# One tile of a pre-LayerNorm block: a transpose on TensorE in place of one by DMA

## The chip, the cores and the metric

The kernel runs on one core of a Trainium2 chip. Its time is the device time of one execution in microseconds; below, "the trace" is one execution recorded by the hardware profiler. Engines are TensorE (PE; its weight loads are listed as PEld), VectorE (DVE), ScalarE (ACT), GpSimd (POOL) and SyncE (SP, which issues most of the DMAs).

## The reference

```python
h  = x + A(layernorm(x))          # linear attention, 32 heads of 32
h2 = h + B(layernorm(h))          # gated ReLU MLP

# A: q, k, v = split(x @ wqkv);  phi(t) = where(t > 0, t + 1, exp(t)) + 1e-6
#    kv = phi(k)^T v ;  z = sum_s phi(k)
#    o  = (phi(q) kv) / (phi(q) z + 1e-6) ;  A = o @ wo
# B: (relu(x @ W_gate) * (x @ W_up)) @ W_down
```

`x` is 1 x 2048 x 1024, `W_gate` and `W_up` are 1024 x 3584, `W_down` is 3584 x 1024, all in bfloat16.

## The kernel before

Tokens are cut into 16 tiles of 128. `order` lists them in two halves of eight: tiles 0 to 3 and 8 to 11 first, then 4 to 7 and 12 to 15. A half has two blocks `hnT[s][0]` and `hnT[s][1]` of 512 tokens each, because the products of the MLP are done by one level of the Strassen-Winograd scheme, seven products in place of eight, for which the two token blocks and the two halves of the feature chunks make a 2 x 2 split. In what follows a tile is named by its place n in `order`, so "tile 7" is `order[7]`, the last of the first half.

The attention's second part goes through each tile in five stages (`attn_stages`): `nd` multiplies by kv and z and divides (matmuls at L511, ScalarE's Ln and Exp at L515 and L517, VectorE's product at L518); `oT` transposes the result by DMA (L525); `x_in` loads the residual (L529); `wo_h` multiplies by `wo` (L541), adds the residual (L543), stores h (L546) and normalises it into the row `hn` (L551 to L557, the last a 128x1024 activation on ScalarE); `hn_T` transposes that row into `hnT` (L560), where the MLP needs the features on the partitions. `LAG = (0, 1, 1, 2, 4)`: at step t the stages of tiles t, t-1, t-1, t-2 and t-4 are written, in this order. The rows `hn` have two buffers.

For the tiles of the second token block, `attn_step` then writes four sums on VectorE (`left_sums`, L117 to L120) that the Strassen products read: `hs` and the rewritten part of `hn`. From step 8 on, four "quads" of the MLP (`early_quad`, products at L705) are woven in between the remaining attention steps: the first product of the first quad at step 8, all others after step 11. A quad's products go to PSUM tags A (two buffers), D (one) and E (two); D is the second product (L705 `Dq`, read by L714). Stage `wo_h` of tiles 6 to 9 borrows tag E, the others take tag `ab`, which has three buffers and is shared with `nd`.

Up to here the order of each engine's instructions is not the order of the code: they are placed by a scheduler when their inputs are ready, earlier code first. After the four quads, the order on PE, VectorE and ScalarE is written out by hand (`quad`, L785 and following).

At the start of the kernel a similar step exists: the first four tiles of the normalised x are transposed by PE (`transpose_in`, L283) into tag D, four 128x128 blocks at a time, and copied to SBUF by VectorE or ScalarE (L284).

Of the kernel before, what the change touches and what calls it, by code (L numbers as in the profile page):

```python
# [10 lines left out]
BF16 = mybir.dt.bfloat16  # L11
# [20 lines left out]
def block_kernel(ctx: ExitStack, tc: tile.TileContext, x, wqkv, wo, wg, wu, wd, out, H: int):  # L32
    nc = tc.nc
    P = 128
    xf = x.flatten_outer_dims()
    of = out.flatten_outer_dims()
    S, D = xf.shape
# [4 lines left out]
    KC = D // P  # L42
# [5 lines left out]
    KH = KC // 2  # L48
# [9 lines left out]
    ident = consts.tile([P, P], BF16, name="ident")  # L58
# [146 lines left out]
    order = [(i * HS + s * SW) // P + tt for s in range(NS) for i in range(2) for tt in range(NT)]  # L205
# [5 lines left out]
    pspool = psctx.enter_context(tc.tile_pool(name="ps", bufs=1, space=PSUM))  # L211
    with ExitStack() as actx:
# [208 lines left out]
        for c in range(KC):  # L421
            bnk, i = divmod(c, GPB)
# [41 lines left out]
    hnT, hns = [], []  # L464
# [32 lines left out]
    def attn_stages(t):  # L497

        i, r = divmod(t * P, HS)
        s, r = divmod(r, SW)  # L500
        st = {}

        def nd():
            o_sb = bwork.tile([P, D], BF16, tag="o_sb", name="o_sb")
            st["o"] = o_sb
            held.append(o_sb)
            ov = o_sb[:].rearrange("p (k h e) -> p k h e", k=KC, h=HPC)
            for c0, n in pieces:
                ps = ndpool.tile([P, NW], FP32, tag="ab", name="nd")
                for c in range(c0, c0 + n):  # L510
                    nc.tensor.matmul(ps[:, (c - c0) * NDW:(c - c0 + 1) * NDW], lhsT=pqT[:, c, t * P:(t + 1) * P],  # L511
                                     rhs=kvz[:, c, :], start=True, stop=True)
                ndv = ps[:, 0:n * NDW].rearrange("p (k w) -> p k w", w=NDW)
                den = bsmall.tile([P, GPB, HPC], FP32, tag="den", name="den")
                nc.scalar.activation(out=den[:, 0:n], in_=ndv[:, :, P:NDW], func=ACT.Ln, bias=deps[:], scale=1.0)  # L515
                rd = bsmall.tile([P, GPB, HPC], FP32, tag="rd", name="rd")
                nc.scalar.activation(out=rd[:, 0:n], in_=den[:, 0:n], func=ACT.Exp, scale=-1.0)  # L517
                nc.vector.tensor_tensor(  # L518
                    out=ov[:, c0:c0 + n], in0=ndv[:, :, 0:P].rearrange("p k (h e) -> p k h e", h=HPC),
                    in1=rd[:, 0:n, :].unsqueeze(3).to_broadcast([P, n, HPC, Dh]), op=ALU.mult)  # L520

        def oT():
            oT = bwork.tile([P, D], BF16, tag="oT", bufs=XB, name="oT")
            st["oT"] = oT[:].rearrange("p (c t) -> p c t", c=KC)
            nc.sync.dma_start_transpose(out=st["oT"], in_=st["o"][:])  # L525

        def x_in():
            x_sb = bwork.tile([P, D], BF16, tag="x_res", bufs=XB, name="x_res")
            nc.sync.dma_start(out=x_sb[:], in_=xf[t * P:(t + 1) * P, :])  # L529
            st["x"] = x_sb  # L530

        def wo_h(borrow):
            h_sb = st["x"]
            tot = bsmall.tile([P, 2], FP32, tag="tot", name="tot")
            for j in range(2):
                if borrow:
                    ps = pspool.tile([P, NW], FP32, tag="E", bufs=2, name="attn")
                else:
                    ps = abpool.tile([P, NW], FP32, tag="ab", name="attn")
                for c in range(KC):  # L540
                    nc.tensor.matmul(ps[:], lhsT=st["oT"][:, c, :], rhs=wo_sb[:, c, j * NW:(j + 1) * NW],  # L541
                                     start=(c == 0), stop=(c == KC - 1))
                nc.vector.scalar_tensor_tensor(out=h_sb[:, j * NW:(j + 1) * NW], in0=ps[:], scalar=1.0,  # L543
                                               in1=h_sb[:, j * NW:(j + 1) * NW], op0=ALU.mult, op1=ALU.add,
                                               accum_out=tot[:, j:j + 1])
            nc.sync.dma_start(out=h_dram[i][s][:, r // P, :], in_=h_sb[:])  # L546
            st["hn"] = bwork.tile([P, D], BF16, tag="hn", bufs=HB, name="hn")

            sm = bsmall.tile([P, 6], FP32, tag="sm", name="sm")
            nmean, var, lnv, rstd, nmr = (sm[:, i:i + 1] for i in range(5))  # L550
            nc.vector.tensor_scalar(out=nmean, in0=tot[:, 0:1], scalar1=tot[:, 1:2], scalar2=-1.0 / D,  # L551
                                    op0=ALU.add, op1=ALU.mult)
            nc.scalar.activation(out=st["hn"][:], in_=h_sb[:], func=ACT.Square, bias=nmean, scale=1.0, accum_out=var)  # L553
            nc.scalar.activation(out=lnv, in_=var, func=ACT.Ln, bias=LN_EPS, scale=1.0 / D)
            nc.scalar.activation(out=rstd, in_=lnv, func=ACT.Exp, scale=-0.5)
            nc.scalar.activation(out=nmr, in_=nmean, func=ACT.Identity, scale=rstd)
            nc.scalar.activation(out=st["hn"][:], in_=h_sb[:], func=ACT.Identity, bias=nmr, scale=rstd)  # L557

        def hn_T():
            nc.sync.dma_start_transpose(out=hnT[s][i][:, :, r:r + P], in_=st["hn"][:])  # L560

        return nd, oT, x_in, wo_h, hn_T

    LAG = (0, 1, 1, 2, 4)
    STS = ST // NS
# [163 lines left out]
    for f in range(NE):  # L729
        st = {}  # L730
# [149 lines left out]
    for r, (wt, f, fi, toks) in enumerate(runs):  # L880
        w = [ops() for _, ops in now]
        later = []
        for n, s in enumerate(toks):
# [51 lines left out]
            if k == nwin - 3:  # L935
                for x in range(2):
                    t = wpools[1].tile([P, KC * 2 * GP * P], BF16, tag=("wg", "wu")[x], name="wd")
# [16 lines left out]
    for n in range(2):  # L954
        t = fpool.tile([P, 4 * D], BF16, tag="wraw", bufs=2, name="xd")
# [242 lines left out]
    for n in range(1, len(OUTER)):  # L1198
# [73 lines left out]
        else:  # L1272
            pss = []
            for p in range(4):
# [13 lines left out]
                s, t0 = divmod(2 * p, NT)  # L1288
# [55 lines left out]
```

## Time and profile before

| | us |
|---|---|
| median of 4 runs | 743.79 (742.24 to 744.88) |
| profiled execution | 744.27 |
| its span, first to last instruction | 742.50 |
| PE busy | 726.7 (98%) |
| VectorE busy | 563.3 (76%) |
| ScalarE busy | 322.1 (43%) |
| DMA issues of `hn` transposes | 16, median 3.7 from issue to landing |

A row of the page or of a timeline names the line of the code, the engine, the operation, and `out<-in` by the program's names. In a timeline the bracket at the end of a row is the time that the engine idled before it, and what ended that. In a table of stretches each engine has its busy time and the number of its instructions, and "PEclk" is the TensorE clock that was granted, 1.00 being the full one.

### The profile page before, as it was taken

Reading aid. Unit: us, or ns where it says so; the run is one execution under the profiler, and the core shown is the slowest. Engines: PE = TensorE matmul, PEld = TensorE weight load, DVE = VectorE, ACT = ScalarE, POOL = GpSimd, SP = SyncE. Lnnn points to the kernel's source line nnn. Section 1 sums busy time; section 2 is a strip of 40 time slices with the busy share of each in tenths; the row PEclk is TensorE's granted clock in tenths of the full one; section 3 lists DMA queues with packets and bytes.
Section 4 is the critical chain, followed back from the end, with each engine's and each line's share of the span. In section 5 each row is a group of like instructions: output and inputs, shape, how many; then the busy total and the mean of one; then the engine's idle time right before and its main releaser. Section 6 shows DMA issues by size and latency. Waiting matters only on the chain.

```text
span 742.5 us, 10623 instructions
## 1 busy us (share of the span) xinstructions
PE 726.7 (98%) x4020; PEld 382.5 (52%) x4020; DVE 563.3 (76%) x991; ACT 322.1 (43%) x580; POOL 5.7 (1%) x44
## 2 busy tenths in 40 slices
PE   8999999999989999999999999999999999999997
PEld 3444555444434444444444444444444458888566
DVE  6998653676987667778778777877787469996797
ACT  4786653878686655444443434443445120000000
POOL 0000000000000000000000000000000000000000
PEclk9999999999999999999999999999999999999999
DMA  9765003079796525164647349475574399988822
GB/s 317 167 140 156 0 1 111 4 162 235 163 212 158 134 79 186 49 191 125 203 134 219 123 164 305 158 207 207 178 265 133 116 393 355 319 289 300 298 77 80
DMA packets 146579, 132.03 MB, mean 178 GB/s; under 512 B 50912, under 2 KB 128096, under 8 KB 146528
## 3 DMA queue, kind: packets, MB, share of 16 engines
q1 hardware_dynamic: 135392, 123.23, 55.1%
q10 hardware_dynamic: 11136, 8.13, 3.4%
q8 instruction: 31, 0.51, 0.3%
q14 instruction: 20, 0.16, 0.1%
HBM read 79.95 MB, written 39.85 MB: 161 GB/s over the span
## 4 chain that ended last, share of the span: by engine, by line
PE 78%; DVE 8%; ACT 7%; DMA 5%; issue 1%; SPq 0%; DVEq 0%; POOL 0%; ACTq 0%
PE accA L785 22%; PE accY L785 8%; PE accX L785 8%; PE accA L1117 8%; PE Aq L298 3%; PE accA L946 3%; PE accX L1117 3%; PE Aq L438 3%; PE accY L1117 2%; PE attn L541 2%; DMA hn<-hn 2%; PE Aq L705 2%; PE Eq L298 2%; PE accY L946 2%; PE accX L946 2%; ACT hn L553 1%
## 5 line engine op out<-in xcount | busy, mean ns | idle before, releaser
L795 ACT ACTIVATE gu<-gu 128x512 bf16<-128x512 bf16 x72 | 45.4, 630 | 131.4 <-DVE gu L794 131.4
L790 ACT COPY snap<-accA 128x1024 f32<-128x1024 f32 x72 | 72.5, 1008 | 36.4 <-PE accA L785 36.3
L785 PEld LDWEIGHTS <-tg 128*128 128x128 f16 x384 | 37.6, 98 | 45.3
L785 PEld LDWEIGHTS <-tu 128*128 128x128 f16 x384 | 37.6, 98 | 45.3
L541 PE MATMUL attn<-wo_mem,oT 128*128 128x512 bf16 x256 | 58.6, 379 | 1.1 <-DMA oT<-o_sb 0.6
L794 DVE TENSOR_TENSOR gu<-accY,snap 128x1024 bf16<-128x1024 f32 x36 | 43.9, 1220 | 10.0 <-ACT snap L790 10.0
L785 PE MATMUL accA<-hn,tg 128*128 128x512 f16 (+1 forms) x192 | 49.3, 379 | 0.0
L785 PE MATMUL accA<-hn,tu 128*128 128x512 f16 (+1 forms) x192 | 49.3, 379 | 0.0
L154 ACT COPY u<-Aq 128x512 f32<-128x512 f32 x56 | 32.4, 582 | 38.5 <-PE Aq L298 19.2
L794 DVE TENSOR_TENSOR gu<-accX,snap 128x1024 bf16<-128x1024 f32 x36 | 43.9, 1220 | 6.3 <-PE accX L785 3.7
L1117 PEld LDWEIGHTS <-x 128*128 128x128 f16 (+1 forms) x448 | 43.8, 98 | 5.5
L785 PEld LDWEIGHTS <-wg 128*128 128x128 bf16 x288 | 28.2, 98 | 34.0
L785 PEld LDWEIGHTS <-wu 128*128 128x128 bf16 x288 | 28.2, 98 | 34.0
L541 PEld LDWEIGHTS <-oT 128*128 128x128 bf16 x256 | 24.7, 98 | 31.3 <-issue 3.1
L798 DVE TENSOR_TENSOR hq<-gu 128x512 bf16<-128x512 bf16 x48 | 20.3, 423 | 14.3 <-ACT gu L795 14.2
L298 PEld LDWEIGHTS <-xT 128*128 128x128 bf16 (+1 forms) x192 | 18.6, 98 | 23.6 <-issue 2.2
L1117 PEld LDWEIGHTS <-xs 128*128 128x128 f16 x280 | 27.4, 98 | 3.2
L543 DVE SCALAR_TENSOR_TENSOR x_res<-attn,x_res 128x512 bf16<-128x512 f32 x32 | 21.8, 688 | 8.6 <-PE attn L541 8.6
L946 PEld LDWEIGHTS <-x 128*128 128x128 bf16 (+1 forms) x168 | 16.4, 98 | 19.6
L518 DVE TENSOR_TENSOR o_sb<-nd,rd 128x384 bf16<-128x384 f32 (+1 forms) x48 | 22.8, 508 | 4.6 <-ACT rd L517 4.5
L1123 DVE TENSOR_TENSOR snap<-accA,u 128x1024 f32<-128x1024 f32 x16 | 19.5, 1221 | 8.3 <-PE accA L1117 8.1
L785 PE MATMUL accA<-hs,tg 128*128 128x512 f16 x96 | 24.6, 379 | 0.0
(232 smaller groups left out, 1407.8 us busy)
## 6 DMA issues: line engine op xcount, KB each, us to landing
x<-x_dram SPq DMA_DIRECT2D x17, 896.0 KB, 8.0
x_dram<-hq SPq DMA_DIRECT2D x28, 512.0 KB, 3.2
wg<-in_B_W_gate_dram SPq DMA_DIRECT2D x14, 512.0 KB, 5.2
wu<-in_B_W_up_dram SPq DMA_DIRECT2D x14, 512.0 KB, 7.3
wraw<-in_B_W_down_dram SPq DMA_DIRECT2D x14, 512.0 KB, 5.1
x_dram<-hq SPq DMA_DIRECT2D x28, 256.0 KB, 2.7
t_dram<-wt SPq DMA_DIRECT2D x28, 256.0 KB, 2.2
xd<-x_dram SPq DMA_DIRECT2D x6, 896.0 KB, 7.1
```

The costliest lines, as they stand in the source:

```text
L154: nc.scalar.copy(out=snaps[nm, v], in_=A[v][:])
L298: nc.tensor.matmul(ps[:], lhsT=left[m - 1][:, kc, r + v * P:r + (v + 1) * P], rhs=right[m - 1][:, kc, :], start=(start and kc == 0), stop= ...
L438: nc.tensor.matmul(ps[:], lhsT=rq[m - 1][:, kc, (c + v) * P:(c + v + 1) * P], rhs=left[m - 1][:, kc, :], start=(start and kc == 0), stop=( ...
L518: nc.vector.tensor_tensor(out=ov[:, c0:c0 + n], in0=ndv[:, :, 0:P].rearrange("p k (h e) -> p k h e", h=HPC), in1=rd[:, 0:n, :].unsqueeze(3 ...
L541: nc.tensor.matmul(ps[:], lhsT=st["oT"][:, c, :], rhs=wo_sb[:, c, j * NW:(j + 1) * NW], start=(c == 0), stop=(c == KC - 1))
L543: nc.vector.scalar_tensor_tensor(out=h_sb[:, j * NW:(j + 1) * NW], in0=ps[:], scalar=1.0, in1=h_sb[:, j * NW:(j + 1) * NW], op0=ALU.mult, ...
L785: nc.tensor.matmul(ps[:, v, :], lhsT=w[v][n - 1][:, kc, :], rhs=left[n - 1][:, kc, :], start=(t is not None and kc == 0), stop=(kc == KH - ...
L790: nc.scalar.copy(out=st[nm][:], in_=halves(st["A"]))
L794: add(out=g[:], in0=halves(st[nm]), in1=st[base][:], op=ALU.add)
L795: nc.scalar.activation(out=g[:, 0, :], in_=g[:, 0, :], func=ACT.Relu)
L946: nc.tensor.matmul(ps[:, t * NW:(t + 1) * NW], lhsT=x_tile(n, s, kh)[:, f, (t0 + t) * P:(t0 + t + 1) * P], rhs=w_tile(n, kh)[:, f, :], sta ...
L1117: nc.tensor.matmul(pv[:, tt, :], lhsT=left(m)[:, f, tt * P:(tt + 1) * P], rhs=right(m)[:, f, :], start=(t is not None and f == 0 and tt % ...
```

## The change

For tile 7 alone, `hn_T` no longer issues a DMA transpose. PE transposes the row's eight 128x128 blocks into one PSUM tile of tag D, ScalarE copies the first four blocks into `hnT` and VectorE the last four. The other fifteen tiles keep their DMA transposes.

```diff
         def hn_T():
+            if t == order[STS - 1]:
+                pt = pspool.tile([P, KC, P], BF16, tag="D", bufs=1, name="tp")
+                for kc in range(KC):
+                    nc.tensor.transpose(pt[:, kc, :], st["hn"][:, kc * P:(kc + 1) * P], ident[:])
+                nc.scalar.copy(out=hnT[s][i][:, 0:KH, r:r + P], in_=pt[:, 0:KH])
+                nc.vector.tensor_copy(out=hnT[s][i][:, KH:KC, r:r + P], in_=pt[:, KH:KC])
+                return
             nc.sync.dma_start_transpose(out=hnT[s][i][:, :, r:r + P], in_=st["hn"][:])
```

## The prediction

> **What bounds the kernel now.** I read the page first, then the stretch table around the edited step, then TensorE's, SyncE's, ScalarE's and VectorE's timelines there, and last the chain of waits. On the page TensorE (PE) is busy 726.7 of 742.5 us, so a change gains only by closing a hole in PE's stream or by raising its clock. The table of stretches shows where a hole is (columns: length, then busy time of PE, weight loads, VectorE, ScalarE, GpSimd, then granted clock, DMA share, GB/s):
>
> ```profile
> 216.95:220.34 3.39, 0.68 (x7) 0.37 (x5) 2.83 (x10) 3.26 (x11) 0.00 (x0) 1.00 0.94 258
> 220.34:223.73 3.39, 2.98 (x8) 1.05 (x8) 3.39 (x10) 1.91 (x6) 0.00 (x0) 0.50 0.97 236
> 223.73:293.00 69.27, 67.51 (x327) 30.80 (x326) 49.22 (x121) 41.09 (x94) 0.00 (x0) 1.00 0.53 139
> 293.00:600.00 307.00, 307.00 (x1424) 139.18 (x1423) 227.15 (x415) 127.26 (x170) 0.00 (x0) 1.00 0.56 176
> ```
>
> PE works 0.68 of 3.39 us, and then 3.39 us pass at a granted clock of 0.50. Afterwards there is always other work: 1.76 us idle up to 293, none up to 600. What is won or lost near 220 is therefore kept to the end. PE's timeline (start, length, instructions, idle time before them in brackets):
>
> ```profile
> 207.79 0.38 PE L705 MATMUL Dq<-hn,wg 128*128 128x512 bf16 x1
> ...
> 212.75 0.59 PE L705 MATMUL Dq<-hn,wg 128*128 128x512 bf16 x2
> 213.23 3.61 PE L541 MATMUL attn<-wo_mem,oT 128*128 128x512 bf16 x16
> 216.68 0.34 PE L511 MATMUL nd<-kvz,pq_mem 128*128 128x132 bf16 x3
> 217.21 0.34 PE L511 MATMUL nd<-kvz,pq_mem 128*128 128x132 bf16 x3 [0.19 <-DVE o_sb L518]
> 218.55 0.28 PE L511 MATMUL nd<-kvz,pq_mem 128*128 128x132 bf16 x2 [1.00 <-DVE o_sb L518]
> 220.75 1.01 PE L705 MATMUL Eq<-hs,tg 128*128 128x512 f16 x2 [1.93 <-DVE hs L117]
> ```
>
> The hole is 0.19 + 1.00 + 1.93 = 3.12 us, and its largest part ends with the first Strassen sum (L117) of the first half's last tile, tile 7 in the order. SyncE, ScalarE and VectorE say why that sum is late:
>
> ```profile
> 216.14 1.46 SPq L560 DMA_TRANSPOSE hn<-hn  x1
> ...
> 212.47 1.24 ACT L557 ACTIVATE hn<-x_res,sm 128x1024 bf16<-128x1024 bf16 x1
> ...
> 218.42 1.24 ACT L557 ACTIVATE hn<-x_res,sm 128x1024 bf16<-128x1024 bf16 x1
> ...
> 219.02 0.69 DVE L543 SCALAR_TENSOR_TENSOR x_res<-attn,x_res 128x512 bf16<-128x512 f32 x1
> ...
> 220.27 0.43 DVE L117 TENSOR_TENSOR hs<-hn 128x512 f16<-128x512 bf16 x1 [0.56 <-DMA hn<-hn]
> ```
>
> Tile 7's normalised row is ready at 213.71 (212.47 + 1.24), its DMA is issued only at 216.14 because it stands behind other issues on SyncE, and it lands at 220.25 (216.14 + 4.11 in the chain of waits). But VectorE idles for it only 0.56 us: until 219.71 its own queue is full. That cuts down what a faster transpose can give.
>
> **The change, part by part.** *Removed:* one DMA transpose, 1.46 us of SyncE's queue. SyncE's next issue starts at 218.52, when the L518 result it reads is complete, so its other transfers gain nothing.
>
> *Added on PE:* eight transposes. The rows of L283, the same operation at the kernel's start, show four in 0.39 us with 219 ns for one: (0.39 - 0.219)/3 = 57 ns apart, so eight in a row take 7 x 0.057 + 0.219 = 0.62 us. They need tile 7's row (213.71) and come after attn of tile 9, which ends at 216.84, or in front of it. Behind it they fill the hole: cost 0. If the hole has been closed by something else they cost 0.46 to 0.78 us.
>
> A rule speaks against the move: the Trainium skill, "VectorE: DVE Perf Modes", section "Rules for kernel authors", gives a 128x128 transpose to TensorE only if PSUM will do as its destination, and the DMA otherwise; its table of transpose paths has 390 ns for one on TensorE. By that figure eight would be an estimated 3.1 us, the whole hole, and the sum would lose its gain. The row of L283 (four in 0.39 us) speaks otherwise, and I go by it.
>
> *Added on VectorE and ScalarE,* since the result must return to SBUF: one 128x512 copy each. Their rows at L284 are 426 ns and 576 ns. VectorE is solid from 216.26 to 219.71; a copy inside that stretch moves the sums by 0.35 us (such a copy at 17.40 lets the next row start at 17.74), one in the idle 1.43 us before 216.26 by nothing. ScalarE is the doubtful one: L553 and L557 of tile 8 hold it from 216.35 to 219.66 but for short gaps between their small operations. In a gap the copy ends near 218.3, behind L557 at 219.66 + 0.58 = 220.24, as late as the DMA.
>
> *Moved:* `pt` shares PSUM tag D, one buffer, with the Strassen result Dq of the first quad. The code asks for `pt` first, so I let the four Dq matmuls at 207.79 to 213.2 wait until `pt` is copied out: 4 x 0.216 = 0.86 us (0.216 from attn: (3.61 - 0.379)/15). Before, they lay in time that PE would have idled, since attn of tile 9 waits for VectorE's L543 anyway; after, they lie in the hole if the copies end by about 219.6, otherwise they cost up to 0.86 us. If Dq keeps the buffer, `pt` waits for its reader L714, which stands at 223.01, behind the sums; that end belongs to the slower case below.
>
> *The waits.* L117 of tile 7 can start at 220.0 with the copy (0.35) behind L543 of tile 9 (219.65), at 219.65 with the copy earlier, and at 219.02 if it goes between the two L543. Against 220.27 that is 0.27 to 1.25 us; I take 0.85, nearer the early end, because VectorE and ScalarE both idle at 214.8 to 216.3 and the transposes can run from 213.75 if they go before attn of tile 9. Behind L117 nothing new is late: L118 to L120 and the L518 of tile 12 follow in the same order.
>
> *The clock.* Of the 3.39 us at 0.50 PE was busy 2.98, so it lost 1.49 us. In the stretch before, PE would be busy 0.68 + 0.62 = 1.30 us with the transposes, 2.16 with Dq too. The nearest row is one from the kernel's start, where PE was busy 1.24 of 3.40 us and no half clock followed:
>
> ```profile
> 5.80:9.20 3.40, 1.24 (x9) 0.65 (x8) 2.35 (x6) 0.27 (x2) 0.00 (x0) 1.00 1.08 355
> ```
>
> 0.20 of a stretch busy led to half clock, 0.36 did not; 0.38 to 0.64 lies on the safe side, so I take the whole 1.49 us as saved, with 0 as the other end.
>
> The Trainium skill, "TensorE: Matmul & The Clock Gate", Part 1, says that the gate goes to half rate after an idle window of about 3.4 us, and that the windows run freely, not from the kernel's start. This trace agrees on the length (3.39 us); that the loss falls in some executions and not in others is something one profile cannot show, and by it the term would be anything from 0 to 1.49.
>
> *Sum:* -0.85 - 1.49 = -2.34 us. The profiled execution took 744.27 us (1.77 around its span of 742.50), so 741.93 by its measure; the median of the runs is 743.79, 0.48 below it, which makes **741.4 us**. A measurement of this kernel tells about 0.3% from no change, 2.23 us: faster is below 741.56, slower above 746.02.
>
> **The rivals.** *Little comes of it.* The copy on ScalarE goes behind L557 of tile 8, L117 starts where it did, and the removed DMA was not what set the end: VectorE's full queue was, for which its idle of 0.56 us speaks. Then the four Dq matmuls stand in front of Eq: PE starts them at 220.2 in place of Eq at 220.75 and is 0.86 - 0.55 = 0.31 us behind. With the clock saved that is -1.2 us, without it +0.3; in the middle -0.4, 743.4 us. Against it: the gaps on ScalarE.
>
> *Slower: the copy on ScalarE falls behind tile 9's normalisation as well.* L553 of tile 9 needs the row buffer that tile 7 frees (two buffers), and in the code it comes before the transpose, so both wait for the same release and L553 (1.15 us) may go first. Then it runs at 220.2, the copy ends near 222.0, L117 follows, Dq and Eq stand from 222.0: 1.25 us more idle, 0.86 for Dq, and the stretch at 0.50 is followed by a second one, of which I count half, 0.75. Together +2.9: 746.7 us. The same price holds if `pt` has to wait for L714. It decides once that copy ends after about 221.3. For it: one release wakes both. Against it: L553 of tile 9 also waits for L551, at 220.62 today.
>
> *More than forecast.* All of the hole and the half clock go: -3.12 - 1.49, plus the transposes 0.62, is -4.0, 739.8 us. VectorE's full queue speaks against it; it is the bound on the gain.
>
> **How the numbers follow.** Forecast with its lower neighbour 0.44: both sides of it (the clock row and the idle engines at 214.8 to 216.3) stand in the trace. Little comes of it 0.30. Slower 0.26, because an order set by readiness is changed next to three full queues and nothing in the trace shows the new order. The likeliest case's own range is 739.8 to 742.4. The range goes from 740.0, which leaves out the bound on the gain, to 746.9, which takes in the middle case and the slower one up to its own time; what is left out is the far half of the slower case, some 0.13, and some 0.04 below.
>
> **What would show it.** Right: no row of PE clock below 1 between 213 and 225, L117 of tile 7 before 220, Dq matmuls after the copies and before Eq, PE idle between 216.9 and 221 below 1.5 us, and 15 DMA transposes of hn in place of 16. Wrong: ScalarE's copy behind a 128x1024 activation of tile 8 or 9, VectorE idle in front of L117 with the releaser ScalarE or PE, a half clock of two windows, or PE standing in front of the transposes because they were queued ahead of attn of tile 9 before the row was ready (0.5 us).

## The result, and the profile after

The changed kernel takes **745.42 us** (median; 744.04 to 747.02 in 35 runs), the kernel before 744.37 in the same session: ratio 1.0015, 95% interval 1.0008 to 1.0022. It is 1.05 us slower: less than the 0.3% that the prediction set as its bound, but the interval leaves out 1. The forecast was a gain of 2.3 us. Executions come with or without a stretch of half clock, about 1.7 us apart: of the 144 runs of the kernel before with a clock on record, 49 have a mean granted clock of 1.000 (median 742.57) and 81 one of 0.997 or 0.998 (744.23). For the changed kernel the two medians are some 744.6 (clock 0.999 or 1.000) and 745.90; at the same clock the change costs 1.7 to 2 us.

The profiled execution took 745.90 us, its span is 744.1. The stretches that answer to those of the prediction (columns as there):

```profile
217.60:221.00 3.40, 1.42 (x17) 1.03 (x16) 3.40 (x12) 3.27 (x10) 0.00 (x0) 1.00 0.50 150
221.00:224.40 3.40, 3.13 (x9) 1.16 (x9) 2.91 (x8) 3.33 (x11) 0.00 (x0) 0.59 1.17 232
224.40:293.00 68.60, 67.11 (x324) 30.64 (x323) 48.24 (x120) 40.16 (x92) 0.00 (x0) 1.00 0.51 136
293.00:600.00 307.00, 306.78 (x1422) 138.94 (x1420) 228.23 (x417) 126.25 (x169) 0.00 (x0) 1.00 0.56 176
```

The hole has moved by 0.65 us and is still there. PE now works 1.42 of 3.40 us in it, and the half clock comes all the same; by the trace's own record of the clock it lasts from 221.63 to 225.05, and in the 3.41 us right ahead of it PE is busy 1.16 us. The last row has lost something too: 306.78 busy of 307.00, where before PE never paused. TensorE's, ScalarE's and VectorE's timelines around the hole:

```profile
214.32 0.23 PE L563 MATMUL tp<-ident,hn 128*128 128x128 bf16 x1 [0.85 <-ACT hn L557]
214.38 3.62 PE L541 MATMUL attn<-wo_mem,oT 128*128 128x512 bf16 x16
217.84 0.55 PE L563 MATMUL tp<-ident,hn 128*128 128x128 bf16 x7
...
221.27 1.11 PE L712 MATMUL Dq<-hn,wg 128*128 128x512 bf16 x3 [1.81 <-DVE hn L565]
```

```profile
219.05 1.24 ACT L557 ACTIVATE hn<-x_res,sm 128x1024 bf16<-128x1024 bf16 x1
220.19 0.56 ACT L564 COPY hn<-tp 128x512 bf16<-128x512 bf16 x1
```

```profile
216.90 0.42 DVE L117 TENSOR_TENSOR hs<-hn 128x512 f16<-128x512 bf16 x1 [1.50 <-DMA hn<-hn]
...
220.26 0.42 DVE L627 TENSOR_TENSOR tg<-wg,tg 128x512 f16<-128x512 bf16 x1
...
220.79 0.42 DVE L565 COPY hn<-tp 128x512 bf16<-128x512 bf16 x1
221.22 0.56 DVE L518 TENSOR_TENSOR o_sb<-nd,rd 128x384 bf16<-128x384 f32 x1
221.70 0.41 DVE L117 TENSOR_TENSOR hs<-hn 128x512 f16<-128x512 bf16 x1
```

One transpose goes ahead of attn of tile 9 and holds PE up for 0.85 us until the row is ready; the other seven come behind it, in 0.55 us. ScalarE's copy stands behind L557 of tile 8, as the middle rival had it. VectorE's copy follows it, and L117 of tile 7 starts 16.47 us behind L117 of tile 4 (221.70 - 205.23); before it was 15.63. So far the trace looks like a plain answer: the result comes back late. That is a part of it; the experiments show that it is not the whole. The first row of VectorE, which has nothing to do with tile 7, counts as well: VectorE idles 1.50 us for tile 6's DMA, as it did before:

```profile
216.26 0.42 DVE L117 TENSOR_TENSOR hs<-hn 128x512 f16<-128x512 bf16 x1 [1.43 <-DMA hn<-hn]
```

From L117 of tile 4 to the first product of L785 (L792 in the changed kernel) the profiled runs take 88.32 us before and 88.92 after; from there to the end of the span 449.54 and 449.95. The rest of the difference in span (1.60), 0.59, is there before L117 of tile 4 starts, where nothing was edited; that point lies between 204.6 and 205.3 in all kernels below that keep the length of the warm-up.

### The profile page after: what moved, and what is told of

It is laid out like the page before. It is cut to its first block, busy times and chain, and to the rows that moved or that the text cites. A ratio compares the mean times of both kernels' runs of the same rounds, so it can differ in the third digit from the quotient of the medians.

```text
span 744.1 us, 10638 instructions
## 1 busy us (share of the span) xinstructions
PE 728.3 (98%) x4028; PEld 383.2 (52%) x4028; DVE 563.5 (76%) x992; ACT 322.6 (43%) x581; POOL 5.7 (1%) x44
## 4 chain that ended last, share of the span: by engine, by line
PE 74%; DVE 10%; ACT 7%; DMA 6%; issue 2%; SPq 0%; DVEq 0%; POOL 0%; ACTq 0%
PE accA L792 21%; PE accA L1124 8%; PE accX L792 8%; PE accY L792 8%; PE Aq L298 3%; PE accA L953 3%; PE accX L1124 3%; PE Aq L438 3%; PE attn L541 3%; PE accY L1124 2%; DMA hn<-hn 2%; PE Eq L298 2%; ACT hn L553 2%; PE accY L953 2%; PE accX L953 2%
## 5 line engine op out<-in xcount | busy, mean ns | idle before, releaser
L792 PEld LDWEIGHTS <-tg 128*128 128x128 f16 x384 | 37.6, 98 | 45.8 <-issue 0.7
L792 PEld LDWEIGHTS <-tu 128*128 128x128 f16 x384 | 37.6, 98 | 45.3
L792 PE MATMUL accA<-hn,tg 128*128 128x512 f16 (+1 forms) x192 | 49.3, 379 | 0.2 <-ACT snap L797 0.2
L792 PE MATMUL accA<-hn,tu 128*128 128x512 f16 (+1 forms) x192 | 49.3, 379 | 0.0
L792 PEld LDWEIGHTS <-wg 128*128 128x128 bf16 x288 | 28.2, 98 | 34.0
L792 PEld LDWEIGHTS <-wu 128*128 128x128 bf16 x288 | 28.2, 98 | 34.0
L518 DVE TENSOR_TENSOR o_sb<-nd,rd 128x384 bf16<-128x384 f32 (+1 forms) x48 | 23.1, 508 | 5.8 <-ACT rd L517 4.1
L792 PE MATMUL accA<-hs,tg 128*128 128x512 f16 x96 | 24.6, 379 | 0.0
```

Source lines behind the costliest of these rows:

```text
L518: nc.vector.tensor_tensor(out=ov[:, c0:c0 + n], in0=ndv[:, :, 0:P].rearrange("p k (h e) -> p k h e", h=HPC), in1=rd[:, 0:n, :].unsqueeze(3 ...
L792: nc.tensor.matmul(ps[:, v, :], lhsT=w[v][n - 1][:, kc, :], rhs=left[n - 1][:, kc, :], start=(t is not None and kc == 0), stop=(kc == KH - ...
```

## First experiments: the parts of the change

Theory 1 is the late result: the two copies stand behind ScalarE's and VectorE's queues. Rivals: the first transpose holds PE up; the PSUM buffer D displaces Dq; what sets the time is not tile 7 at all but tile 6's DMA; and the clock alone. Times below are medians, with the ratio to the kernel before on the same chip and its 95% interval. Line numbers are those of each kernel.

**One copy in place of two.**

```diff
-                nc.scalar.copy(out=hnT[s][i][:, 0:KH, r:r + P], in_=pt[:, 0:KH])
-                nc.vector.tensor_copy(out=hnT[s][i][:, KH:KC, r:r + P], in_=pt[:, KH:KC])
+                nc.vector.tensor_copy(out=hnT[s][i][:, :, r:r + P], in_=pt[:])
```

> The changed kernel, with both halves of the transposed tile copied to SBUF by one 128x1024 copy on VectorE, none on ScalarE. Theory A (the result of the transposes comes back too late: ScalarE's copy stands behind the 128x1024 activation of tile 8, and VectorE's copy waits for ScalarE's): the copy starts directly behind the two L543 of tile 9, L117 of tile 7 starts 0.5 to 0.9 us earlier than in the changed kernel, and the time is 0.4 to 1.0 us below the changed kernel's. Theory B (the first transpose, queued ahead of attn of tile 9, holds PE 0.85 us): nothing moves, since that transpose stays where it is; 0 +- 0.3 us. Theory C (the PSUM buffer D: the displaced Dq matmuls cost 0.86 us): nothing moves either.

Measured: 746.01 us, 1.0028 (1.0015 to 1.0040). L117 of tile 7 is back at 15.83 us behind L117 of tile 4, 0.64 earlier than in the changed kernel, and the time is not better. An earlier sum that gains nothing speaks against theory 1 as the whole answer, though not cleanly: this run has stalls of its own, PE idle 1.53 us at 267.7 and 0.58 at 615.1.

**The transposes in another PSUM tag,** so that Dq keeps its place.

```diff
-                pt = pspool.tile([P, KC, P], BF16, tag="D", bufs=1, name="tp")
+                pt = abpool.tile([P, KC, P], BF16, tag="ab", name="tp")
```

> The changed kernel, with the transposes' PSUM tile in tag ab (three buffers) in place of D, so that Dq can run early again, and no transpose stands ahead of attn of tile 9. Theory A: the copies still come back behind tile 8's activation on ScalarE, L117 of tile 7 no earlier than in the changed kernel, time within 0.4 us of it. Theory B: PE's 0.85 us in front of the first transpose are gone, 0.6 to 0.9 us below the changed kernel. Theory C: Dq is back at its early place, and the time is back at the kernel before, 1.1 us below the changed kernel.

Measured: 746.46, 1.0033 (1.0020 to 1.0047). Dq is back in its old place and the time is no better, so nothing speaks for the rival of the buffer. This run too has a stall elsewhere, 2.40 us of PE at 268.

**All transposes behind attn of tile 9.**

```diff
-                for kc in range(KC):
-                    nc.tensor.transpose(...)
+                with tc.issue_after(last_attn[order[STS + 1]].ins):
+                    for kc in range(KC):
+                        nc.tensor.transpose(...)
```

> The changed kernel, with all eight transposes kept behind the last matmul of attn of tile 9 on PE; the order of every other instruction is as in the changed kernel. Theory A: PE is no longer idle in front of the first transpose, but VectorE's queue is set by the landing of tile 6's DMA and not by that, so L117 of tile 7 starts where it did and the time is within 0.3 us of the changed kernel's. Theory B: 0.6 to 0.9 us below it. Theory C: no difference.

Measured: 745.63, 1.0019 (1.0004 to 1.0034). The 0.85 us of PE in front of attn had no price that shows.

**Tile 7 by DMA as before, but ahead on SyncE's queue** (`tc.high_priority()` around the DMA).

> The kernel before, with tile 7's DMA transpose issued ahead of the residual load and the store of h that stood before it on SyncE; the order on PE, VectorE and ScalarE is unchanged. If the DMA's place in SyncE's queue sets the stall: it is issued near 214 in place of 216.1, lands near 218, L117 of tile 7 starts behind L543 of tile 9 at 219.65, 0.6 us earlier, and the time is 0.4 to 0.7 us below the kernel before, 2 us if the half clock goes too. If VectorE's full queue sets it (the part of theory A that holds for the DMA as well): 0 to 0.6 us below it, with the half clock still there.

Measured: 743.91, 0.9998 (0.9987 to 1.0009).

**The kernel before with four matmuls of 128x512 in the hole** that nobody reads, ahead of the last `nd` group of tile 12.

> The kernel before, with four 128x512 matmuls put in front of the last group of nd of tile 12, in the hole; they write a PSUM bank that nd then overwrites, so only time is added. PE works 0.86 us more in the hole. If the half clock follows from how little PE did in the stretch before it (20% busy in the kernel before, now 45%), it is gone and the section from tile 4's L117 to the first L785 matmul falls from 88.3 to about 86.8 us, the time by 1 to 1.5 us. If 45% is still too little (42% was, in the changed kernel, there with 128-column matmuls), the half clock stays and the section is 88.3 +- 0.3 us.

Measured: 742.91, 0.9995 (0.9981 to 1.0009); 7 of 12 runs at a clock of 1.000, two at 0.999.

**PE transposes tile 6 instead of tile 7** (`order[STS - 2]`), without and with tile 7's DMA ahead on SyncE's queue; and **both tiles by DMA, both ahead**.

> The changed kernel's edit on tile 6 in place of tile 7: tile 6 is transposed by PE, tile 7 by DMA. New theory D (the stall was set by tile 6's DMA, which lands at 216.3 and makes VectorE idle 1.43 us with everything after it queued behind, and not by tile 7's): VectorE's idle time in front of tile 6's L117 goes, L117 of tile 7 starts at its own DMA's landing or about 1 us earlier, the hole is 1 to 1.4 us shorter, minus 0.5 us for the transposes; 0.5 to 1 us below the kernel before, 2 more if the half clock goes. Theory E (any such transposes cost their PE time and a reorder, whichever tile they are for): 0.3 to 1.5 us above the kernel before, as in the changed kernel.

> Tile 6 transposed by PE and tile 7's DMA transpose issued ahead of the load and the store in front of it on SyncE; same order on PE, VectorE and ScalarE as with tile 6 alone. Theory D: both waits of VectorE (1.43 and 0.56 us) shrink; PE's hole is under 2 us, and the time is 0.3 to 0.8 us below that with tile 6 alone. Theory E: 0.3 to 1.5 us above the kernel before.

> The kernel before, with the DMA transposes of tiles 6 and 7 issued ahead of the residual loads and stores of h that stood before them on SyncE; PE's and ScalarE's order unchanged. Theory D: tile 6's DMA lands about 1 us earlier, VectorE idles 0.4 in place of 1.4 us for it, the hole falls from 3.1 to about 2 us and the section from 88.3 to about 87.3 us (85.8 if the half clock goes). If the landing time (5.3 us, the longest) and not the issue sets it: section 88.1 us as with tile 7 alone.

Measured: 744.91, 1.0014 (1.0000 to 1.0027); 744.41, 1.0003 (0.9990 to 1.0015); 743.67, 0.9995 (0.9980 to 1.0011).

Read together these runs fall into two groups, whatever the edit: all kernels with more PE instructions than before pause PE somewhere between 550 and 616 us, far from the edit, and the two with the old number (tile 7 ahead, both tiles ahead) do not. In the changed kernel it is here (VectorE, then weight loads and matmuls of PE):

```profile
547.86 0.69 DVE L657 TENSOR_TENSOR wt<-wraw 128x1024 f16<-128x1024 bf16 x1 [3.31 <-issue]
```

```profile
553.28 0.53 PEld L792 LDWEIGHTS <-tg 128*128 128x128 f16 x3 [0.24 <-issue]
...
555.38 1.02 PE L792 MATMUL accA<-hn,tg 128*128 128x512 f16 x4 [0.22 <-ACT snap L797]
555.38 0.53 PEld L792 LDWEIGHTS <-tg 128*128 128x128 f16 x3 [0.50 <-issue]
```

In the kernel before, the same wait of VectorE is shorter and PE does not pause:

```profile
546.03 0.69 DVE L650 TENSOR_TENSOR wt<-wraw 128x1024 f16<-128x1024 bf16 x1 [2.67 <-issue]
```

Matmuls start 216 ns apart there; in the changed kernel two starts are 342 and 601 ns behind the one before, 0.51 us too much.

What VectorE waits for is a DMA, and among the transfers of that stretch stands one that no line of the kernel issues (the changed kernel's DMA queues, 544.6 to 547.7: packets, MB, share of 16 engines' time):

```profile
q1 hardware_dynamic: 1065, 1.17, 105.3%
q8 instruction: 1, 0.02, 2.0%
```

The page counts 31 such packets in either kernel. Each is 16 KB, takes 0.9 to 2.3 us (most of them about 1.1) and comes once in some 25 us; the PE and PEld rows count 8040 instructions before, one packet for about 256 of them. So this queue carries PE's instructions. The change adds eight transposes and their eight weight loads, and so shifts the later packets. The trace's record of DMA completions, 16 pieces to a transfer, shows what that does to the transfer that ends VectorE's wait:

| kernel | PE's packet | 15th piece | 16th piece |
|---|---|---|---|
| before | 546.97 to 548.03 | 545.84 | 545.86 |
| changed | 546.70 to 547.70 | 546.99 | 547.68 |
| four pads in the hole | 544.13 to 545.08 | 544.20 | 545.05 |

Where the packet falls into the transfer, one of its 16 pieces ends with the packet. All twenty profiles of this case agree for this transfer: in the eight whose packet is under way when the 16th piece lands, that piece comes 0.40 to 0.89 us behind the 15th; in the other twelve, 0.01 to 0.18. The reverse does not hold: other transfers have a late last piece with no packet near (in the kernel before, 359.79 and 360.56).

The Trainium skill, "Runtime: NRT & Kernel Launch", section "Instruction fetch mechanics", says that an engine's instructions are refilled in 16 KiB blocks of 256 by a DMA queue of its own, and calls the cost of a block boundary mostly hidden. The 31 packets agree with the first. Whether PE itself ever waits for a block, no run here measures; what the table adds is a cost beside PE, a block's transfer that holds up another one.

## Second experiments: the number of instructions alone

Theory 2: the change's time is that of its own plus that of the moved packets. The kernel's 16 warm-up matmuls on zeros, at the start of PE's stream, let the number of instructions be changed without any work near the hole.

**Sixteen instructions more, nothing else.**

```diff
-            for n in range(SPIN):
-                nc.tensor.matmul(spin[:], lhsT=zero[:, 0:P], rhs=zero[:], start=True, stop=True)
+            for n in range(24):
+                nc.tensor.matmul(spin[:, 0:340], lhsT=zero[:, 0:P], rhs=zero[:, 0:340], start=True, stop=True)
```

> The kernel before, with one edit at its very start: the 16 warm-up matmuls of 512 columns on zeros become 24 of 340 columns, so TensorE's stream holds 16 more instructions (8 matmuls, each with its weight load), as many as the change adds, and nothing else of any engine's order is touched. Theory 1 (instruction fetch): TensorE's instructions come in packets of 16 KB, 31 in the run, on the DMA engines, each about 1.0 us on one engine. In the kernel before the packet of 546.97 us comes 1.1 us after the store of wt, for which VectorE waits at L650 (2.67 us idle), has landed (15 of 16 pieces by 545.84, the last at 545.86). In the changed kernel the packet starts at 546.70, its 15 pieces are in at 546.99 and the sixteenth only at 547.68, where the packet ends; VectorE idles 3.31 us there and TensorE pauses 0.13 + 0.39 us near 553 and 555. So with 16 instructions more the same happens here: VectorE's wait at L650 3.2 to 3.4 us, the last piece 0.6 to 0.9 us behind the fifteenth, 0.4 to 0.6 us of pauses of TensorE near 551 to 553, the median 0.5 us above the kernel before (ratio 1.0007). Theory 2 (the pause comes from the rearranged hole at 213 to 224 us, or from chance in the landing): wait 2.6 to 2.8 us, no pause, ratio 1.0000.

Measured: **745.21**, 1.0023 (1.0011 to 1.0035): as much as the whole change costs, and more than expected. At 545.6 to 546.0 the sixteenth piece is 0.40 behind, and matmuls start 0.25 us late at 553.22. Two more places are hit that the changed kernel does not have. Behind 613.22 the next matmul starts 0.95 us later, where the others are 0.11 apart, and at 262.42 the packet falls into a DMA transpose: 15 pieces by 262.89, the last at 264.49. VectorE, then PE:

```profile
264.51 0.42 DVE L117 TENSOR_TENSOR hs<-hn 128x512 f16<-128x512 bf16 x1 [2.39 <-DMA hn<-hn]
```

```profile
267.80 1.02 PE L705 MATMUL Aq<-hs,tu 128*128 128x512 f16 x4 [2.64 <-ACT m L154]
```

In the kernel before these two rows are:

```profile
264.76 0.42 DVE L117 TENSOR_TENSOR hs<-hn 128x512 f16<-128x512 bf16 x1 [0.51 <-DMA hn<-hn]
```

```profile
268.05 1.02 PE L705 MATMUL Aq<-hs,tu 128*128 128x512 f16 x4 [0.72 <-ACT m L154]
```

The stall at the same place in three first experiments is of the same kind: the tag ab kernel and both with tile 6 on PE have their packet at 265.04, 262.19 and 261.21, in the flight of that transpose, and PE idles 2.40 to 2.41 us. For the 1.53 us of the one-copy kernel no such packet is shown.

**The changed kernel with 56 more** (44 warm-up matmuls of 186 columns).

> The changed kernel with 44 warm-up matmuls of 186 columns in place of 16 of 512: 56 more instructions of TensorE at the start (four matmuls of the first 20 us change places with each other, nothing else). Theory 1: the fetch packet that starts at 546.70 in the changed kernel comes some 5 us earlier, ahead of the stretch in which the transfers run at their full rate (from 544.0), and holds no piece up: VectorE's wait at L657 is 2.6 to 2.8 us instead of 3.31, the last piece within 0.1 us of the fifteenth, the two pauses of TensorE near 553 and 555 are gone, and the median lies 0.5 us below the changed kernel's: 744.9, ratio to the kernel before 1.0008. Theory 2: wait 3.2 to 3.4 us and pauses as in the changed kernel, ratio 1.0015. The hole at 213 to 224 stays as in the changed kernel under both: L117 of tile 7 about 16.5 us behind L117 of tile 4.

Measured: 745.79, 1.0024 (1.0009 to 1.0039): not the gain expected. At 548 no piece is late any more (15th 548.26, 16th 548.28) and the pauses at 553 are gone, but behind 616.03 the next matmul starts 0.91 us later, and the profiled run has half clock from 9.9 to 13.3 us, behind the narrower warm-up. Moving the packets by an arbitrary amount changes one hit for another.

**The kernel before with eight 128x128 matmuls in the hole** that nobody reads: as many PE instructions as in the changed kernel, ahead of the hole and behind it, with tile 7 by DMA.

```diff
+                for c in range({6: 8}.get(c0, 0) if t == order[12] else 0):
+                    nc.tensor.matmul(ps[:, 0:P], lhsT=pqT[:, 0, t * P:(t + 1) * P], rhs=wo_sb[:, 0, 0:P],
+                                     start=True, stop=True)
```

> The kernel before, with eight matmuls of 128x128 that nobody reads put ahead of the last nd group of tile 12, in TensorE's hole behind Dq: TensorE does as much more work as the eight transposes are (16 instructions), but tile 7 still comes by DMA and nothing waits for them. If the transposes' own work costs something though they lie in a hole: the section from L117 of tile 4 to the first L785, without TensorE's idle time and the loss at half clock, grows from 81.8 us by 0.3 to 0.5; if not, by under 0.1. Theory 1 (fetch) adds the pause of 0.5 us near 551 to 553 in any case. Late result (the copies come back behind L557 of tile 8 and VectorE's queue): that is absent here, L117 of tile 7 stays about 15.6 us behind L117 of tile 4 (16.47 in the changed kernel), and the profiled run at the same granted clock is 0.5 to 1.2 us below the changed kernel's. If the late result costs nothing, it equals the changed kernel: ratio 1.0015. Half clock: filled hole with 128-column matmuls, so as in the changed kernel it can come or not.

Measured: **745.56**, 1.0024 (1.0013 to 1.0036). The work of eight transposes, with the DMA kept, costs more than the change does. But the pair is not a clean one: at the hole the packets fall alike (214.13 and 213.68), later one comes at 262.95 here and at 267.91 in the changed kernel, and here it meets a DMA transpose (15 pieces by 263.38, the last at 264.95; VectorE idles 2.34 us). So an equal number of instructions does not make the packets come at equal moments.

**The number of before, in the changed kernel.** Four fp32 warm-up matmuls, recorded as eight with eight weight loads, replace 16 bf16 ones. That is 16 instructions fewer at the start for the 16 of the transposes; behind the hole as many instructions have gone by as before, ahead of it 16 fewer. Its control is the kernel before with the same edit.

```diff
-            for n in range(SPIN):
-                nc.tensor.matmul(spin[:], lhsT=zero[:, 0:P], rhs=zero[:], start=True, stop=True)
+            z32 = zero[:].bitcast(FP32)
+            for n in range(4):
+                nc.tensor.matmul(spin[:].rearrange("p (o n) -> p o n", o=2), lhsT=z32[:, 0:P],
+                                 rhs=z32.unsqueeze(1).to_broadcast([P, 2, NW // 2]), start=True, stop=True)
```

> The changed kernel with 4 warm-up matmuls in fp32 (512 columns, four instructions of TensorE each) in place of 16 in bf16 (two each): TensorE's stream is 17 instructions shorter than the changed kernel's and one shorter than that of the kernel before, so that behind the hole every instruction packet is fetched at the same instruction as in the kernel before. Every engine's order is otherwise that of the changed kernel. Fetch theory: no piece late at 546 to 548 (VectorE's wait at L657 2.6 to 2.8 us instead of 3.31), no pauses of TensorE at 553 and 555, the stall of Aq near 268 at 0.4 to 0.8 us, and the median 0.5 us or more below the changed kernel: 744.9 or less, ratio 1.0008 or less. What then is left above 1.0000 is the price of the late result. Late-result theory alone: ratio 1.0015 as in the changed kernel. L117 of tile 7 stays some 16.5 us behind L117 of tile 4 under both.

> Control: the kernel before with the same 4 fp32 warm-up matmuls, 16 instructions fewer than before and every order as before. Each packet behind the start is fetched some 1.7 us later. Fetch theory: the one of 546.97 moves further away from the landing of 545.86, no pause near 553; the one of 268.96 moves away from the landing of 264.7; the one of 600.93, in front of an x load that lands at 601.0 with its last piece 0.4 us behind the fifteenth, moves behind it, which can only help: ratio 0.9990 to 1.0000. The one of 213.2 moves to 215 and may hold up tile 6's or tile 7's transpose (16.2 to 218.4): up to 1 us more, ratio up to 1.0010. If the warm-up in fp32 matters by itself, the first 30 us show it.

Measured: **742.02, 0.9973** (0.9960 to 0.9985), and 743.87, 1.0005 (0.9991 to 1.0018) for the control. With its instructions taken back elsewhere the change comes with a gain of 1.9 us, more than theory 2 had expected; the next views point to the packet ahead of the hole. VectorE and PE at the hole, and the two stretches:

```profile
215.34 0.43 DVE L117 TENSOR_TENSOR hs<-hn 128x512 f16<-128x512 bf16 x1
...
220.15 0.41 DVE L117 TENSOR_TENSOR hs<-hn 128x512 f16<-128x512 bf16 x1
```

```profile
219.72 0.81 PE L714 MATMUL Dq<-hn,wg 128*128 128x512 bf16 x3 [0.91 <-DVE hn L567]
```

```profile
217.60:221.00 3.40, 2.49 (x23) 1.55 (x22) 3.39 (x11) 3.40 (x10) 0.00 (x0) 1.00 0.64 122
221.00:224.40 3.40, 3.40 (x17) 1.56 (x16) 3.38 (x11) 1.94 (x6) 0.00 (x0) 1.00 1.21 235
```

No wait for tile 6 is left, PE idles 0.91 us in front of Dq in place of 1.81, and the clock stays at 1.00. Tile 6's DMA transpose, issued near 211 in all kernels, tells why (issues: median us to landing is the last number; the kernel before, the changed one, and this one):

```profile
hn<-hn SPq DMA_TRANSPOSE x1, 5.3
```

```profile
hn<-hn SPq DMA_TRANSPOSE x1, 5.5
```

```profile
hn<-hn SPq DMA_TRANSPOSE x1, 4.0
```

With PE's packet in its flight (213.23 before, 213.68 changed, 214.13 in the kernel with eight pads) it takes 5.3 to 5.7 us; with the packet at 215.5 to 215.7 it takes 3.9 to 4.1. Here all 16 pieces come late, not one. Over the fourteen profiles that leave tile 6's DMA in its place, VectorE idles 1.43 to 1.78 us for it in the eight with a packet between 213.2 and 214.4, and 0 to 0.47 in the other six. So the 1.43 us of the kernel before, and with it a part of the hole, go with a packet of instructions.

**The same, with all transposes behind attn of tile 9.**

> The version with all transposes of tile 7 behind attn of tile 9 (1.0019 as it stood), with the 4 fp32 warm-up matmuls, so that its fetches fall as in the kernel before. Fetch theory: 0.5 to 0.6 us off the median, the pause near 552 gone: 745.0, ratio 1.0010 or less. If the first transpose that stands ahead of attn of tile 9 in the changed kernel (0.85 us of TensorE) has a price of its own, it lies 0.5 to 0.9 us below g1_b4; if not, the same within 0.3.

Measured: 741.90, 0.9969 (0.9957 to 0.9981), the same as 742.02 within 0.3: the transpose in front of attn costs nothing that shows.

**Is the gain the change's or the packets'?** Tile 7 by DMA, eight unread matmuls in the hole, four fp32 warm-up matmuls: as many instructions as in the kernel of 742.02, ahead of the hole and behind it, within one.

> The kernel before, with 4 fp32 warm-up matmuls in place of 16 and eight matmuls of 128x128 that nobody reads in TensorE's hole: the same number of TensorE's instructions ahead of the hole and behind it as in g1_b4 (742.02, 0.9973), within one, but tile 7 comes by DMA. If the gain of g1_b4 is that of the fetches alone, it comes out the same: ratio 0.996 to 0.9985. If it is the change's own, as the step of the prediction on L117 of tile 7 and the half clock had it, the packet of 213 us, 215.5 here, falls on tile 7's DMA as in g2_b4 (issued at 215.09, VectorE idle 1.33 us for it, L117 at 219.6), TensorE's hole stays open and takes the half clock in part of the runs, and the time is that of g2_b4 or the kernel before, 743.5 to 744.5, ratio 0.9995 to 1.0008: 1.5 to 2.5 us above g1_b4.

Measured: **743.61, 1.0000** (0.9990 to 1.0011). So the gain is not the packets' alone: at the same number, and with the packet at the hole alike (215.45 and 215.69), the change is worth 1.6 us. Much of that is the clock: seven of the eight runs at 742.02 have the full clock, and five of the twelve here; among these the medians are 741.90 and 742.79, 0.9 us apart (on two chips). Part of the rest may again be a packet: it now falls into the flight of tile 7's DMA, the very transfer that the change takes away. VectorE, then PE:

```profile
215.10 0.43 DVE L117 TENSOR_TENSOR hs<-hn 128x512 f16<-128x512 bf16 x1
220.02 0.42 DVE L117 TENSOR_TENSOR hs<-hn 128x512 f16<-128x512 bf16 x1 [1.48 <-DMA hn<-hn]
```

```profile
220.50 1.01 PE L710 MATMUL Eq<-hs,tg 128*128 128x512 f16 x2 [2.39 <-DVE hs L117]
```

**Versions to beat both.** Both tiles' DMAs ahead on SyncE's queue and four 128x512 pads in the hole, with three warm-ups: 44 matmuls of 186 columns; 12 of 512, which takes the eight instructions of the pads back; 8 of 512 and two in fp32, which does so at full length.

> A version meant to be better than both: the kernel before, with the DMA transposes of tiles 6 and 7 issued ahead of the loads and stores on SyncE's queue, four matmuls of 128x512 that nobody reads in TensorE's hole (which took the half clock out of 7 of 12 runs where it stood alone), and 44 warm-up matmuls of 186 columns, which bring the instruction fetch of 547 us well ahead of the landing it would hit. Fetch theory: no pause near 551 to 553, VectorE's wait there 2.6 to 2.8 us. Sum: section 86.0 to 87.0 us (88.32 before), the half clock in fewer executions, median 742.0 to 743.0, ratio 0.998. If clock and fetch do not matter, ratio 0.9995, as the two moved DMAs alone gave.

> The version with the DMA transposes of tiles 6 and 7 ahead on SyncE's queue and four padding matmuls of 128x512 in the hole, with 12 warm-up matmuls instead of 16: eight instructions fewer at the start for the eight of the padding, so that behind the hole the fetches fall as in the kernel before. The run with 44 warm-up matmuls gave 742.99 (0.9988), with a pause of 0.34 us at 611 and the start of the section 1.5 us late. Expected: no pause at 611, no start lost, section 84.5 to 85.5 us without half clock, median 741.0 to 742.0, ratio 0.9965 to 0.9975. If the shorter warm-up lets the clock fall at the start, that shows before 15 us.

> The version with the DMA transposes of tiles 6 and 7 ahead on SyncE's queue and four padding matmuls, with 8 warm-up matmuls in bf16 and 2 in fp32 (eight instructions fewer for the eight of the padding, and the warm-up as long as before). g3_both_spin12 had 742.38 with one stretch of half clock at 9.0 to 12.9 us, behind its shorter warm-up, and L117 of tile 4 at 205.94 instead of 204.6 to 205.1. Expected: no half clock there, L117 of tile 4 at 205.0, section 84.9, median 741.0 to 741.6, ratio 0.996 to 0.9975, below g1_b4's 742.02.

Measured: 742.99, 0.9988 (0.9977 to 0.9999), with PE idle 0.28 us near 611; 742.38, 0.9982 (0.9973 to 0.9990), a miss of 0.4 us, since the shorter warm-up is followed by half clock from 9.2 to 12.6; and **740.96, 0.9966** (0.9952 to 0.9979), with neither. The last, from six runs, has the lowest median here, though its interval overlaps those of the two kernels at 742.02 and 741.90. It needs no transpose on PE.

## Why the prediction was wrong, step by step

| step | predicted | changed kernel | with the number of instructions of before |
|---|---|---|---|
| L117 of tile 7, from L117 of tile 4 (before: 15.63) | -0.85 | +0.84 | -0.54 |
| the same, from L117 of tile 6 (before: 4.01) | -0.85 | +0.79 | +0.80 |
| half clock at the hole | -1.49 | not saved | saved |
| profiled execution (744.27) | -2.34 | +1.63 | -2.13 |
| median | -2.4 | +1.05 | -1.90 |

- **L117 (-0.85 in the sum): the step that failed in its own terms.** The prediction let the transposes run from 213.75, ahead of attn of tile 9, and the copies in the idle time that ends at 216.3. One transpose ran ahead; the other seven came behind attn, until 218.39, and both copies behind that. VectorE does not idle once between L117 of tile 6 (216.90) and L117 of tile 7 (221.70), and its order is a new one: L627, the copy and an L518 stand ahead of L117, of which L627 (L620 there) and L518 stood behind it before. "Behind L117 nothing new is late" looked at the wrong side. The distance is 4.80 us in place of 4.01, and 4.81 where tile 6's DMA is in time, so this loss is the change's own and not the packets'.
- **The transposes at no cost.** Their own time was sized well (0.62; the seven in a row took 0.55), but they did not fill the hole: from 8 to 20 us behind L117 of tile 4, PE idles 3.10 us where it idled 3.12 before. The first one holds PE up for 0.85, and Dq, pushed into the hole, waits 1.81 for the copy.
- **The clock (-1.49).** The prediction read busy shares over stretches that do not lie where the chip's do. In the kernel before, the full clock lasts 215.04 us and the half clock 3.413: 63 windows and one. Cut at such marks, the twenty profiles of this case have 13 windows of half clock ahead of the end. The window before each had PE busy for 0.21 to 0.46 of it; all eleven windows up to 0.424 were followed by half clock, two of the four from 0.429 to 0.456, and none above. By these marks the row of 5.80 to 9.20 (0.36, no half clock) is one of 5.28 to 8.69 with 0.52, so the "safe side" began too low, and the changed kernel's 0.34 (1.16 of 3.41) lies where half clock always followed. The Trainium skill, "TensorE: Matmul & The Clock Gate", Part 4, says that work in transpose mode does not count as busy in the same way for the gate; no run here tests that, and of the seven transposes at most 0.17 us (218.22 to 218.39) lies in that window. Over all runs the full clock came in 19 of 36 of the changed kernel (49 of 144 before, 7 of 8 with the instructions taken back).
- **What is not in the sum at all: the added instructions.** The prediction had no term for the packets that carry PE's instructions, though the page lists their queue. Sixteen instructions alone cost as much as the change (1.0023), and the 1.43 us of VectorE's wait for tile 6's DMA, taken as free room for the copies, went with a packet in that transfer's flight; in the changed kernel it is there again (1.50).
- **-2.13 for -2.34 in the last column is luck in its terms.** L117 comes 0.54 earlier there because tile 6's wait is gone, not because tile 7's transpose is faster: the controls with tile 7 by DMA and the packet alike have it at 14.83 and 15.24 us, the change at 15.09. What the change brings there is less idle time of PE (1.89 us from 8 to 20 us behind L117 of tile 4; 2.74 and 2.51 in the controls) and, with it, the full clock.
- **The copies.** ScalarE's went behind L557 of tile 8 and VectorE's behind that, as the middle rival said, and VectorE's full queue, its reason, is what the trace shows. With tile 6 in time ScalarE's copy runs at 218.65 in place of 220.19, its place in the queue the same.
- **Dq behind the copies, the first transpose ahead of attn:** both happened as named. Undoing either changed the time by nothing that shows in its favour.
- **The case that came** is the middle one ("little comes of it") by its mechanism. Its price without the clock saved was +0.3; the measured +1.05 lies between that and the slower case (+2.9).

Open: what the change is worth where the packet meets neither tile's DMA; no run has that. The nearest for the DMA is the kernel with 24 warm-ups (packet from 210.73 to 211.66): VectorE idles 0.47 and 0.62 us for the two DMAs, and L117 of tile 7 stands 14.82 us behind L117 of tile 4, earlier than with the transposes on PE. Open too is why the packet holds up one piece in 16 of some transfers and all pieces of the DMA transpose at 211, and by what rule the moment of a packet is chosen; the runs move packets and do not remove them. For the late matmuls at 613 to 616 the packet as the cause is only argued: in the one-copy version the load that VectorE waits for has its 15th piece at 602.50 and its 16th at 603.55, 1.2 us behind the end of the packet (602.35).

## What to carry to other kernels

In a long unrolled kernel an edit that adds or removes instructions of one engine moves its later instruction packets, and where a packet fell into a transfer that somebody waited for, an engine idled 0.5 to 1.9 us more here. So try an edit at more than one number of instructions (a control with padding alone, or the same edit with padding taken away) before believing a gain or loss below half a per cent. When VectorE or PE waits for a DMA that takes a microsecond longer than its sisters, look in the list of queues for an instruction packet beside it; and before a hole is called safe for the clock, lay the marks of the clock's windows over it.

## What was not expected of the hardware

- One packet of PE's instructions is 16 KB, 0.9 to 2.3 us. The transfers here that it held up had their last piece 0.4 to 1.6 us behind the other fifteen; a DMA transpose of 128x1024 landed in 5.3 to 5.7 us in place of 3.9 to 4.1.
- In the twenty profiles half clock followed every window of 3.413 us with PE busy for up to 0.424 of it, and none above 0.456.
- Eight 128x128 transposes are cheap on PE: seven in 0.55 us, one alone in 0.23.
- Sixteen instructions on zeros in the first 7 us changed the time of a 744 us kernel by 0.23%.
